# Windowed attention and two FFNs: float32 scores, and a new order of work around the transposes of P

## The chip, the cores and the metric

One core of one Trainium2 chip. The metric is the time of one execution on the device in microseconds. The engines are TensorE (PE in the profile, its weight loads PEld), VectorE (DVE), ScalarE (ACT), GpSimd (POOL) and SyncE (SP).

## What is computed

Sixteen heads (2 batches of 8) of 768 positions and 64 elements attend to the last 128 positions and to 4 sink positions at the start; the result, 1536 rows of 512, goes through two FFNs of width 2048. All inputs but the two sizes are float32 or float64, the output is float32.

```python
scores = scale * np.matmul(q, k.transpose(0, 1, 3, 2))
keep = (pos[None, :] < n_sink) | ((rel >= 0) & (rel < window))   # rel = query - key
scores = np.where(keep, scores, -1e9)
a = softmax(scores)
x = matmul(a, v)                       # to (B*S, H*D)
h = x @ w_in;  x = where(h >= 1, h, where(h <= -1, 0, (h + 1)**2 / 4)) @ w_out
h = x @ w2_in; out = (np.maximum(h, 0.0)**2) @ w2_out
```

## The kernel before

**Units.** Attention is cut into 24 units: a batch, a pair of heads `c` and a block `j` of 256 queries (`UNITS`). The two heads of a unit lie on partitions 0 to 63 and 64 to 127; a unit has two halves `u` of 128 queries. The steps of a unit are: loads of q and k (`q`) and of v (`v`); a key tile that takes over the last 128 keys and the sink columns of the block before (`k`, lines 366 to 375: one copy by SP's DMA queue, one POOL copy); the transposes of q and k on PE and their copies to SBUF (`t`, lines 377 to 398); the scores of each half with mask, maximum and exponential (`s0`, `s1`, lines 400 to 435); the norm (`n`, lines 437 to 453: an addition and a reciprocal on DVE, a product per half on POOL, and for j > 0 a small POOL copy per half of the probabilities of the sinks); the transposes of P for each head (`x0`, `x1`, lines 455 to 468) and of the sink columns (`xs`, lines 470 to 483, for j > 0 only), each copied out by ACT; and the product with V (`a`, lines 485 to 504), which for j > 0 begins with one matmul of the sink tile and then takes the two heads in turn, 64 columns of the array each.

**Number formats.** `turn` writes q and k transposed as two float32r parts: ACT casts the PSUM tile (line 394), DVE subtracts the cast from the tile (line 395). A head's scores are then three float32r matmuls (high x high, high x low, low x high: `SPLIT`), 64 rows of the array per head, heads taking turns (lines 410 to 419). A score block has 260 columns: 128 older keys, 4 sinks, 128 own keys; the first block of a sequence has 128. The product with V and all transposes are plain float32. The FFNs use float32r with the same split; their weights come as float64 and are split by ACT, DVE and POOL (`Weights.part`, lines 112 to 133).

**Order.** `fast_path` makes a list of events: step `nm` of unit `n` stands at `n + ORDER[nm]`; to it come the jobs that load or split FFN weights (`JOBS`: per key two loads, then two splits) and the first six FFN steps of 256 positions (`STEPS`). The list is sorted and issued; a planner then gives each engine its instructions by what is ready in its own reckoning, earlier events first. So FFN matmuls run between attention's from 34 us on. PSUM holds two score tiles (`SCB`), one of turned q and k, two of turned P, one for values and two for the FFN; SBUF holds four key tiles (`KB`), three units' P (`PB`) and two units' turned P (`PTB`). After attention the rest of the FFNs runs alone.

Of the kernel before, what the change touches and what calls it, by code (L numbers as in the profile page):

```python
# [8 lines left out]
F32 = mybir.dt.float32  # L9
F32R = mybir.dt.float32r  # L10
# [3 lines left out]
ALU = mybir.AluOpType  # L14
# [3 lines left out]
P = 128  # L18
# [7 lines left out]
NS = 4  # L26
WIN = 2 * P + NS
SLOT = P + NS
# [14 lines left out]
JOBS = [  # L43
    x + d
    for x in (
        3.64, 4.16, 4.68, 5.21, 5.73, 6.26,
        6.78, 7.30, 7.83, 7.83, 8.07, 8.31,
    )
    for d in (0, 0.01)
]  # L50
ORDER = dict(
    q=-1.74, k=-2.06, v=-1.14, s0=-0.59, s1=0.18, t=-0.86, n=1.23, x0=1.40, xs=1.69, x1=1.96, a=2.41,
)
STEPS = [
    (t, (n // 3, n % 3 * 256, 256)) for n, t in enumerate((13.7, 14.0, 17.6, 21.0, 21.2, 21.8))
]
CUTS = ((0, 2, 5, 8, 12, 16), (0, 4, 8, 12, 16))
PASSES = [
# [2 lines left out]
SPLIT = ((0, 0), (0, 1), (1, 0))  # L61


def f32(ap):
    return ap.bitcast(F32)
# [266 lines left out]
class Attention:  # L332
# [32 lines left out]

    def keys_before(self, b, j, c):
        nc = self.nc
        kt = self.po["k"].tile([P, 2, 5, SLOT], F32R, tag="k", name=f"k_{b}_{j}_{c}")
        if j > 0:
            old = f32(self.kt[b, j - 1, c])  # L370
            nc.sync.dma_start(f32(kt)[:, :, 0, :P], old[:, :, 2, :P])
            nc.gpsimd.tensor_copy(
                kt[:, :, 0:2, P:], old[:, :, 1, P:].unsqueeze(2).broadcast_to([P, 2, 2, NS])
            )
        self.kt[b, j, c] = kt

    def turn(self, b, j, c):
        nc, po, kt = self.nc, self.po, self.kt[b, j, c]
        banks = 2 if po["tag"] == "f" else 1
        ps = [  # L380
            po["tp"].tile([P, 4, P], F32, tag=po["tag"], name=f"tp_{b}_{j}_{c}_{i}")
            for i in range(banks)
        ]
        for a, src in enumerate("kq"):
            for u in range(2):
                nc.tensor.transpose(  # L386
                    ps[a % banks][:, 2 * a + u],
                    self.loads.raw[src, b, j, c][:, u].rearrange("p h d -> p (h d)"),
                    self.ident,
                )  # L390
        for i in range(banks):
            blocks = slice(4 * i // banks, 4 * (i + 1) // banks)
            src, dst = ps[i][:, blocks], kt[:, :, 1:, :P][:, :, blocks]
            nc.scalar.copy(dst[:, 0], src)
            nc.vector.tensor_tensor(dst[:, 1], src, f32(dst[:, 0]), ALU.subtract)
        if j == 0:
            nc.gpsimd.tensor_copy(kt[:, :, 1, P:], f32(kt[:, :, 1, :NS]))
        self.st[b, j, c] = dict(nm=f"{b}_{j}_{c}")

    def scores(self, b, j, c, u):  # L400
        nc, po, st = self.nc, self.po, self.st[b, j, c]
        kt = self.kt[b, j, c]
        keys = kt.rearrange("p s n w -> p s (n w)")
        k0 = SLOT if (j == 0 or u == 1) else 0
        wid = P if j + u == 0 else WIN
        ps = [
            po["sc"].tile([P, 512], F32, tag="s", name=f"s_{st['nm']}_{u}_{e}")[:, :wid]
            for e in range(2)
        ]
        for n, (a, bb) in enumerate(SPLIT):  # L410
            for e in range(2):
                pr = slice(64 * e, 64 * e + 64)
                nc.tensor.matmul(  # L413
                    ps[e],
                    kt[pr, a, 3 + u, :P],
                    keys[pr, bb, k0 : k0 + wid],
                    start=n == 0,
                    stop=n == 2,
                )
        if u == 0:  # L420
            st["p"] = [
                po["p"].tile([P, 2, WIN], F32, tag="p", name=f"p_{st['nm']}_{i}") for i in range(2)
            ]
            st["sm"] = po["sm"].tile([P, 3, 2, 2], F32, tag="sm", name=f"sm_{st['nm']}")
        s, sm = st["p"][u][:, :, :wid], st["sm"]
        mask = self.masks[min(2 * j + u, 2)][:, :wid]
        for e in range(2):
            nc.vector.tensor_tensor_reduce(  # L428
                s[:, e], ps[e], mask, -SCALE, 3.0e38, ALU.add, ALU.min, sm[:, 0, u, e : e + 1]
            )  # L430
        for e in range(2):
            nc.scalar.activation(  # L432
                s[:, e], s[:, e], AF.Exp, bias=sm[:, 0, u, e : e + 1], scale=-1.0,
                accum_out=sm[:, 1, u, e : e + 1],
            )
# [360 lines left out]
```

## Time and profile before

| | us |
|---|---|
| median of 3 runs | 685.02 (684.73 to 685.83) |
| profiled execution | 684.93 |
| its span | 682.8 |
| PE busy in the span | 666.5 |
| DVE, ACT, POOL busy | 426.0, 337.9, 295.7 |
| attention's last score matmul starts | 170.6 |
| the last matmul of a product with V starts | 182.1 |

Times in the rows count from the span's start. PE's printed durations reach from a matmul's start to its modelled end and overlap; what a group of matmuls takes from the engine is read from its start to the start of the next row. A plain float32 matmul stands in the trace as two records, a float32r one as one.

### The profile page before, as it was taken

How to read it: one execution, taken by the hardware profiler on the slowest of the kernel's cores; microseconds unless marked ns; L12 is line 12 of the kernel's file. 1: busy time of each engine (PE TensorE's matmuls, PEld its weight loads, DVE VectorE, ACT ScalarE, POOL GpSimd, SP SyncE). 2: the span in 40 equal slices, each digit the busy share in tenths (PEclk: the TensorE clock that was granted, in tenths of full speed). 3: DMA queues.
4: the chain of work that ended last, by engine and by line, in shares of the span. 5: the costliest groups of instructions: out<-in, count | busy, mean ns of one | idle time of the engine just before them, and what ended most of it. 6: DMA issues, size and time to landing. Idle time of an engine off the chain costs nothing.

```text
span 682.8 us, 9689 instructions
## 1 busy us (share of the span) xinstructions
PE 666.5 (98%) x3438; PEld 540.5 (79%) x3438; DVE 426.0 (62%) x885; ACT 337.9 (49%) x727; POOL 295.7 (43%) x302
## 2 busy tenths in 40 slices
PE   7989999999999999999999999999999999999996
PEld 5667777878888888888888878888888888888885
DVE  4788799675479777777677866663566356222221
ACT  4879787765455545445444555453444354122210
POOL 2365655444245444444436577353344344233111
PEclk7999999999999999999999999999999999999999
DMA  4857353210222222222211221221123010000111
GB/s 111 215 140 163 102 124 102 70 32 1 83 76 86 67 84 72 86 69 68 87 61 62 92 63 32 93 85 39 52 74 92 32 61 1 0 1 11 51 62 67
DMA packets 66393, 49.00 MB, mean 72 GB/s; under 512 B 40096, under 2 KB 60832, under 8 KB 66336
## 3 DMA queue, kind: packets, MB, share of 16 engines
q1 hardware_dynamic: 65792, 48.17, 24.5%
q8 instruction: 29, 0.48, 0.3%
q14 instruction: 28, 0.23, 0.1%
q10 hardware_dynamic: 544, 0.13, 0.1%
HBM read 43.04 MB, written 3.15 MB: 68 GB/s over the span
## 4 chain that ended last, share of the span: by engine, by line
PE 84%; DVE 6%; DMA 2%; POOL 2%; ACT 2%; issue 2%; SPq 1%; POOLq 0%; ACTq 0%; DVEq 0%
PE o L212 36%; PE h L178 34%; PE s L413 5%; PE av L501 4%; PE tx L463 3%; PE tp L386 1%; DVE t L187 1%; POOL x L223 1%; DVE wx L128 1%; SPq L322 1%; PE ts L476 1%; DVE u L188 1%; DMA wraw<-in_moe_w_in_dram 1%; POOL w L133 1%; DVE wx L126 1%
## 5 line engine op out<-in xcount | busy, mean ns | idle before, releaser
L178 PE MATMUL h<-x,w 128*128 128x512 f32 (+1 forms) x1272 | 277.7, 373 | 0.0
L178 PEld LDWEIGHTS h<-x,w 128*128 128x128 f32 x1272 | 224.5, 188 | 45.5 <-DVE sm L440 0.4
L212 PE MATMUL o<-g,w 128*128 128x512 f32 (+1 forms) x696 | 144.0, 359 | 1.9 <-POOL g L190 1.1
L133 POOL TENSOR_TENSOR w<-wx,w 128x512 fp32r<-128x512 f32 x64 | 83.3, 1302 | 134.2 <-ACT w L132 132.1
L212 PEld LDWEIGHTS o<-g,w 128*128 128x128 f32 x696 | 116.1, 188 | 25.4 <-POOL g L190 1.5
L212 PE MATMUL o<-w,g 128*128 128x512 f32 (+1 forms) x588 | 135.2, 389 | 0.0
L212 PEld LDWEIGHTS o<-w,g 128*128 128x128 f32 x588 | 109.0, 188 | 24.4
L196 POOL TENSOR_TENSOR g<-t,g 128x512 fp32r<-128x512 f32 x48 | 64.2, 1337 | 103.4 <-ACT g L195 86.7
L190 POOL TENSOR_TENSOR g<-u,g 128x512 fp32r<-128x512 f32 (+1 forms) x58 | 71.0, 1226 | 63.6 <-issue 31.1
L235 DVE TENSOR_TENSOR acc<-o,acc 128x512 f32<-128x512 f32 (+1 forms) x105 | 58.5, 577 | 59.0 <-PE o L212 58.8
L132 ACT CAST w<-wx 128x512 fp32r<-128x512 f32 x64 | 39.7, 621 | 94.9 <-DVE wx L131 75.2
L126 DVE TENSOR_SCALAR wx<-wx 128x512 f32<-128x512 f32 x64 | 38.2, 598 | 55.4 <-ACT wx L124 55.4
L194 DVE SCALAR_TENSOR_TENSOR t<-h,u 128x512 f32<-128x512 f32 x48 | 33.1, 689 | 63.0 <-ACT u L193 36.3
L448 POOL TENSOR_TENSOR p<-p,sm 128x520 f32<-128x520 f32 (+1 forms) x48 | 48.1, 1022 | 46.6 <-DVE sm L441 29.0
L193 ACT ACTIVATE u<-h 128x512 f32<-128x512 f32 x48 | 28.6, 596 | 66.6 <-PE h L178 66.6
L124 ACT ACTIVATE wx<-wraw 128x512 f32<-128x512 f32 x64 | 42.8, 669 | 33.5 <-POOL w L133 29.6
L128 DVE SCALAR_TENSOR_TENSOR wx<-wraw,wx 128x512 int32<-128x512 int32 x64 | 58.4, 913 | 1.0
L432 ACT ACTIVATE p<-p,sm 128x260 f32<-128x260 f32 (+1 forms) x96 | 47.4, 495 | 17.3 <-DVE sm L428 16.3
L187 DVE SCALAR_TENSOR_TENSOR t<-u 128x512 f32<-128x512 f32 (+1 forms) x58 | 43.5, 751 | 18.9 <-ACT u L186 18.9
L413 PE MATMUL s<-k 64*128 64x260 f32 (+1 forms) x288 | 50.3, 324 | 4.8 <-DVE sm L428 3.2
L428 DVE CUSTOM_DVE_ANT_0 p<-s,mask 128x260 f32<-128x260 f32 (+1 forms) x96 | 37.6, 401 | 25.5 <-PE s L413 21.3
L131 DVE CUSTOM_DVE_ANT_0 wx<-wx,wy 128x1024 uint16<-128x1024 uint16 x64 | 50.8, 794 | 1.2
(69 smaller groups left out, 595.5 us busy)
## 6 DMA issues: line engine op xcount, KB each, us to landing
wraw<-in_moe_w_in_dram SPq DMA_DIRECT2D x32, 512.0 KB
wraw<-in_moe_w_out_dram SPq DMA_DIRECT2D x32, 512.0 KB
vr<-in_v_dram SPq DMA_DIRECT2D x24, 128.0 KB
qr<-in_q_dram SPq DMA_DIRECT2D x22, 128.0 KB
kr<-in_k_dram SPq DMA_DIRECT2D x22, 128.0 KB
out_dram<-acc SPq DMA_DIRECT2D x11, 256.0 KB
k<-k SPq DMA_DIRECT2D x16, 128.0 KB
qr<-in_q_dram SPq DMA_DIRECT2D x4, 64.0 KB
```

The lines of the kernel that those rows point to most:

```text
L128: nc.vector.scalar_tensor_tensor(xi, hi, -(1 << 31), xi, ALU.bitwise_and, ALU.bitwise_or)
L131: nc.vector.tensor_tensor(xi, xi, yi, ALU.add)
L133: nc.gpsimd.tensor_tensor(w[:, 1], x, f32(w[:, 0]), ALU.subtract)
L178: nc.tensor.matmul(h, w[:, a, c * P : (c + 1) * P], x[:, b, c, sl], start=n == 0, stop=n == 11)
L187: nc.vector.scalar_tensor_tensor(t, u, 1.0, u, ALU.min, ALU.mult)
L190: nc.gpsimd.tensor_tensor(g[:, 1], u, f32(g[:, 0]), ALU.subtract)
L196: nc.gpsimd.tensor_tensor(g[:, 1], t, f32(g[:, 0]), ALU.subtract)
L212: nc.tensor.matmul(o, lhs, rhs, start=n == 0, stop=n == m - 1)
L235: self.nc.vector.tensor_tensor(dst, o, dst, ALU.add)
L413: nc.tensor.matmul(ps[e], kt[pr, a, 3 + u, :P], keys[pr, bb, k0 : k0 + wid], start=n == 0, stop=n == 2,)
L432: nc.scalar.activation(s[:, e], s[:, e], AF.Exp, bias=sm[:, 0, u, e : e + 1], scale=-1.0, accum_out=sm[:, 1, u, e : e + 1],)
L448: nc.gpsimd.tensor_tensor(s, s, r, ALU.mult)
```

## The change

The keys and queries are kept as one float32 tile: `turn` has one DVE copy out of PSUM in place of the cast on ACT and the subtraction on DVE, the copies of `keys_before` move half the bytes, and a head's scores are one float32 matmul, head 0 first. In the order of work x1 (the second head's transposes of P) comes next to x0, ahead of xs; the norm, x0, the keys, v and s0 move a little; the weight jobs come later, and one of the FFN steps changes its place.

```diff
--- before.py
+++ after.py
@@ -43,16 +43,16 @@
 JOBS = [
     x + d
     for x in (
-        3.64, 4.16, 4.68, 5.21, 5.73, 6.26,
-        6.78, 7.30, 7.83, 7.83, 8.07, 8.31,
+        4.00, 4.50, 5.05, 5.58, 6.10, 6.63,
+        7.15, 7.67, 8.20, 8.44, 8.68, 9.47,
     )
     for d in (0, 0.01)
 ]
 ORDER = dict(
-    q=-1.74, k=-2.06, v=-1.14, s0=-0.59, s1=0.18, t=-0.86, n=1.23, x0=1.40, xs=1.69, x1=1.96, a=2.41,
+    q=-1.74, k=-2.19, v=-1.12, s0=-0.63, s1=0.18, t=-0.86, n=0.94, x0=1.30, xs=1.94, x1=1.37, a=2.41,
 )
 STEPS = [
-    (t, (n // 3, n % 3 * 256, 256)) for n, t in enumerate((13.7, 14.0, 17.6, 21.0, 21.2, 21.8))
+    (t, (n // 3, n % 3 * 256, 256)) for n, t in enumerate((13.7, 14.0, 17.6, 21.7, 21.2, 22.0))
 ]
 CUTS = ((0, 2, 5, 8, 12, 16), (0, 4, 8, 12, 16))
 PASSES = [
@@ -365,12 +365,12 @@
 
     def keys_before(self, b, j, c):
         nc = self.nc
-        kt = self.po["k"].tile([P, 2, 5, SLOT], F32R, tag="k", name=f"k_{b}_{j}_{c}")
+        kt = self.po["k"].tile([P, 5, SLOT], F32, tag="k", name=f"k_{b}_{j}_{c}")
         if j > 0:
-            old = f32(self.kt[b, j - 1, c])
-            nc.sync.dma_start(f32(kt)[:, :, 0, :P], old[:, :, 2, :P])
+            old = self.kt[b, j - 1, c]
+            nc.sync.dma_start(kt[:, 0, :P], old[:, 2, :P])
             nc.gpsimd.tensor_copy(
-                kt[:, :, 0:2, P:], old[:, :, 1, P:].unsqueeze(2).broadcast_to([P, 2, 2, NS])
+                kt[:, 0:2, P:], old[:, 1, P:].unsqueeze(1).broadcast_to([P, 2, NS])
             )
         self.kt[b, j, c] = kt
 
@@ -390,33 +390,26 @@
                 )
         for i in range(banks):
             blocks = slice(4 * i // banks, 4 * (i + 1) // banks)
-            src, dst = ps[i][:, blocks], kt[:, :, 1:, :P][:, :, blocks]
-            nc.scalar.copy(dst[:, 0], src)
-            nc.vector.tensor_tensor(dst[:, 1], src, f32(dst[:, 0]), ALU.subtract)
+            nc.vector.tensor_copy(kt[:, 1:, :P][:, blocks], ps[i][:, blocks])
         if j == 0:
-            nc.gpsimd.tensor_copy(kt[:, :, 1, P:], f32(kt[:, :, 1, :NS]))
+            nc.gpsimd.tensor_copy(kt[:, 1, P:], kt[:, 1, :NS])
         self.st[b, j, c] = dict(nm=f"{b}_{j}_{c}")
 
     def scores(self, b, j, c, u):
         nc, po, st = self.nc, self.po, self.st[b, j, c]
         kt = self.kt[b, j, c]
-        keys = kt.rearrange("p s n w -> p s (n w)")
+        keys = kt.rearrange("p n w -> p (n w)")
         k0 = SLOT if (j == 0 or u == 1) else 0
         wid = P if j + u == 0 else WIN
         ps = [
             po["sc"].tile([P, 512], F32, tag="s", name=f"s_{st['nm']}_{u}_{e}")[:, :wid]
             for e in range(2)
         ]
-        for n, (a, bb) in enumerate(SPLIT):
-            for e in range(2):
-                pr = slice(64 * e, 64 * e + 64)
-                nc.tensor.matmul(
-                    ps[e],
-                    kt[pr, a, 3 + u, :P],
-                    keys[pr, bb, k0 : k0 + wid],
-                    start=n == 0,
-                    stop=n == 2,
-                )
+        for e in range(2):
+            pr = slice(64 * e, 64 * e + 64)
+            nc.tensor.matmul(
+                ps[e], kt[pr, 3 + u, :P], keys[pr, k0 : k0 + wid], start=True, stop=True
+            )
         if u == 0:
             st["p"] = [
                 po["p"].tile([P, 2, WIN], F32, tag="p", name=f"p_{st['nm']}_{i}") for i in range(2)
```

## Rows read from the trace of the kernel before

**Rows 1.** The page, part 1: busy us, share of the span, instructions.

```profile
PE 666.5 (98%) x3438; PEld 540.5 (79%) x3438; DVE 426.0 (62%) x885; ACT 337.9 (49%) x727; POOL 295.7 (43%) x302
```

**Rows 2.** Busy time by stage; columns: stretch, us, engines (instructions), PEclk, DMA share, GB/s.

```profile
0.00:20.00 20.00, 15.62 (x79) 12.60 (x80) 9.66 (x48) 8.38 (x25) 6.26 (x21) 0.74 0.56 127
20.00:45.00 25.00, 21.62 (x147) 15.49 (x147) 20.96 (x67) 21.91 (x66) 12.93 (x24) 0.95 0.67 177
45.00:187.00 142.00, 140.84 (x1039) 111.83 (x1036) 102.42 (x316) 99.95 (x284) 69.37 (x99) 1.00 0.34 86
187.00:675.00 488.00, 486.84 (x2167) 399.18 (x2166) 291.69 (x453) 207.71 (x354) 207.18 (x159) 1.00 0.19 59
```

**Rows 3.** Timeline of PE: start us, duration us, line, operation, tiles, shape, count.

```profile
22.11 0.84 PE L413 MATMUL s<-k 64*128 64x260 f32 x3
...
61.52 0.62 PE L413 MATMUL s<-k 64*128 64x260 f32 x3
62.08 0.44 PE L463 MATMUL tx<-ident,p 128*128 128x128 f32 x2
62.44 0.87 PE L501 MATMUL av<-pt,vr 128*64 128x256 f32 x8
63.24 0.74 PE L178 MATMUL h<-x,w 128*128 128x256 f32 x4
...
170.24 0.62 PE L413 MATMUL s<-k 64*128 64x260 f32 x3
```

**Rows 4.** Timeline of PE, 137.0 to 139.3 us.

```profile
137.04 0.64 PE L413 MATMUL s<-k 64*128 64x260 f32 x6
137.61 0.55 PE L463 MATMUL tx<-ident,p 128*128 128x128 f32 x3
137.91 0.36 PE L501 MATMUL av<-sink_t,vs 96*128 96x256 f32 x1
138.20 1.09 PE L501 MATMUL av<-pt,vr 128*64 128x256 f32 x12
139.22 0.55 PE L463 MATMUL tx<-ident,p 128*128 128x128 f32 x3
```

**Rows 5.** Timeline of PE, 152.3 to 155.4 us.

```profile
152.38 3.14 PE L178 MATMUL h<-x,w 128*128 128x256 f32 x24
155.36 0.38 PE L463 MATMUL tx<-ident,p 128*128 128x128 f32 x2
```

**Rows 6.** Timeline of PE, 109.3 to 112.3 us.

```profile
109.39 0.38 PE L501 MATMUL av<-sink_t,vs 96*128 96x256 f32 x1
109.71 0.65 PE L501 MATMUL av<-pt,vr 128*64 128x256 f32 x2
110.29 0.97 PE L212 MATMUL o<-g,w 128*128 128x256 f32 x6
111.19 1.08 PE L501 MATMUL av<-pt,vr 128*64 128x256 f32 x10
112.20 0.62 PE L413 MATMUL s<-k 64*128 64x260 f32 x3
```

**Rows 7.** Timeline of PE, 120.3 to 120.9 us.

```profile
120.36 0.55 PE L413 MATMUL s<-k 64*128 64x128 f32 x3
120.83 0.66 PE L463 MATMUL tx<-ident,p 128*128 128x128 f32 x4
```

**Rows 8.** Groups by line and shape: count, busy us, mean ns, idle before and releaser.

```profile
L395 DVE TENSOR_TENSOR k<-tp,k 128x512 fp32r<-128x512 f32 x23 | 15.6, 679 | 0.9 <-ACT k L394 0.9
L394 ACT CAST k<-tp 128x512 fp32r<-128x512 f32 x23 | 13.3, 579 | 4.0 <-PE tp L386 3.7 <-PE s L413 0.2
...
L233 DVE COPY acc<-o 128x512 f32<-128x512 f32 x16 | 10.7, 682 | 7.5 <-PE o L212 7.5
```

**Rows 9.** Timeline of PE, first and last broken product with V that has sinks.

```profile
76.62 0.36 PE L501 MATMUL av<-sink_t,vs 96*128 96x256 f32 x1
...
176.05 0.36 PE L501 MATMUL av<-sink_t,vs 96*128 96x256 f32 x1
```

**Rows 10.** Line 371 on SP: operation, count, duration ns min/median/max, first and last us.

```profile
L371 SPq EVENT_SEMAPHORE  x24: 17/28/5364, 8.4 to 129.2; - x24
```

## Prediction

> **What bounds the kernel now.** I read the page first: TensorE is marked busy 98% of the span [rows 1]. That alone does not say where an edit pays, so I cut the span by stage [rows 2]; the granted clock is 0.74 up to 20 us, a mix of 1.2 and 2.4 GHz, and 2.4 GHz from 45 us on. From 187 us to 675 us only the two FFN products run, 2167 matmuls in 488 us; the diff touches nothing there. Attention lies in the first 187 us. Up to 45 us TensorE is idle for 7.8 us (4.4 before 20 us, 3.4 after); from 45 us to 187 us it is idle for 1.2 us of 142, because FFN matmuls of the first steps fill every hole. DVE (102 us) and ACT (100 us) have room in that stage. So from 45 us on the time is the sum of what each visit to TensorE costs, and an engine beside it matters only where it changes how the visits fall.
>
> The third view is the order of TensorE's own work, where I take a visit's price from its start to the start of the next row (the printed durations overlap). Scores of one head, three float32r matmuls of 260 columns, cost 0.55 us [rows 3]. The scores of both heads, side by side in rows 0-63 and 64-127 of the array, cost 0.57 us together [rows 4]. Twenty-four FFN matmuls in a row cost 2.98 us, 0.124 each [rows 5], but six of them between two visits to a part of the array cost 0.90 us [rows 6] instead of 0.74. So a visit that splits in two pays its own fill and drain again and about 0.16 us more around it. This kernel is bound, in the stage that the diff touches, by the number of such visits.
>
> The Trainium skill, TensorEngine Tiling, section Key Properties, says that a change of tiling mode drains TensorE. The 0.90 against 0.74 us fits that; it adds no term of its own.
>
> **The score matmuls.** Removed: three float32r matmuls per head; added: one float32 matmul, which the trace shows as two records. No float32 matmul of 64 rows is in this trace. The nearest row is the float32 visit of one head in the product with V: two records of 256 columns, 0.58 us up to the next row [rows 6]. Four more columns and a 128-column weight load make it about 0.59, against 0.55: +0.035 us a visit. The trace has 37 visits of one head with 260 columns, the first at 22.1 us and the last at 170.2 [rows 3], and 16 of both heads as in [rows 4]: 53 x 0.035 = +1.9 us. For 128 columns, three records cost 0.47 us [rows 7]; two float32 transposes of 128 columns ahead of another part-array visit cost 0.36 [rows 3]. That is -0.11 us for ten visits, -1.1 us. The remaining heads' scores lie in early or broken visits; I leave them alone. The sum is +0.8 us.
>
> What could move it is whether float32 heads still run side by side. 0.58 less 0.36 is 0.22 for two records of 128 columns more, so a float32 record takes 0.11 us for each 128 columns. Eight records of the product with V would take 4 x 0.22 + 4 x 0.11 = 1.32 us in a row, and took 0.80 [rows 3]: in columns, float32 heads do share. If in rows they don't, the 16 joint visits cost 0.59 + 0.44 = 1.03 us for 0.57, +7.4 us. Below nothing only the 128-column visits lead, by 1.1 us: no row shows one head's float32 visit of 256 columns under 0.58. I take +0.8, since float32r scores already share by rows.
>
> The Trainium skill, FP8 and Floating Point Precision, section TensorE Precision Notes, says that true float32 takes four passes through the array. The two records of 0.22 us, beside 0.12 us for a float32r pass of as many columns, agree. By the rule alone, four passes for three, each of the 53 visits pays 0.12 us more, an estimate, +6.4 us; the row has less because a float32 visit waits less for its weights.
>
> **The keys.** Removed: the ACT cast of each turned tile, 23 of them of 579 ns [rows 8], 13.3 us, and with it one hop in the chain transposes, cast, subtraction, scores. The DVE subtraction (679 ns) becomes a DVE copy out of PSUM; the nearest such copy takes 682 [rows 8], so DVE is unchanged. The POOL copies of the sink columns and the SP copies of the old keys have half the bytes. From 45 us on, ACT's 13.3 us are hidden: TensorE has other work. From 20 to 45 us ACT is busy 21.9 of 25 us and DVE 21.0 [rows 2], so for the five units that pass there 5 x 0.58 = 2.9 us come off the fullest engine. Against it, up to 20 us the lower clock [rows 2] doubles what float32 streams more (0.44 for 0.36): +0.16 us for some six visits, +1.0. Bounds: -2.9 and +1.0 us; I take -1.0, the middle, since DVE is next to late there and keeps its work.
>
> **The order of work.** The numbers in ORDER are places in units; the planner issues what is ready, in this order. x1 (the second head's transposes of P) goes from 1.96 to 1.37, beside x0; xs (the sink columns) goes behind both, from 1.69 to 1.94; values stay at 2.41. Today the product with V often starts when only the first head's P is turned: sink and two records, then FFN work, then the other ten, 0.90 + 1.01 = 1.91 us [rows 6], where an unbroken visit takes 1.31 [rows 4]. With 0.16 for the fragment between, a broken product costs 0.76 us more. There are ten: seven with sinks, the first at 76.6 us and the last at 176.0 [rows 9], and three without. The product's first matmul needs the sink tile, which is now turned last, so both heads should be ready by then. I count six of the ten as mended: 6 x 0.76 = -4.6 us; bounds 0 and -7.6.
>
> The moved steps' other instructions: the norm (1.23 to 0.94) puts two small DVE and two to four POOL instructions ahead of the next unit's turn and second scores; POOL is busy 69 of 142 us [rows 2], so it is hidden. The keys step (-2.06 to -2.19) puts its SP copy ahead of the loads of V and 0.13 units nearer to the tile that it reads; SP's waits at that line are 28 ns in the median and 5.4 us at most [rows 10], and V is wanted over three units later: nothing. The jobs that load and split weights come 0.34 to 0.6 units later, the last pair 1.16. That takes splits out of the full stretch before 45 us and puts them where they are covered; FFN work has its first weights a little later. I count both at nothing. The steps that change places (21.7 before: 21.0) are filler at the end of attention, nothing.
>
> **Sum.** The profiled execution took 684.9 us with a span of 682.8, and the median of the runs is 685.0. 684.9 + 0.8 - 1.0 - 4.6 = 680.1. Own range 676 to 684.
>
> **The rivals.**
> *More joint visits.* Shorter keys and a freer order could let more scores find both PSUM banks free. Each pair of single visits that joins saves 0.55 + 0.55 + 0.16 - 0.59, about 0.7 us. Ten of 37 singles make five joint visits, all of them 18: -3.5 to -12.6 us, 667.5 to 676.6. For it: sixteen already find both banks free. Against it: the two banks still come free one DVE reduction after the other.
> *Broken visits (slower).* In the new cycle the next scores (0.37), x1 (0.37) and values (0.41) fall together behind x0 (0.30), all in different parts of the array, and a score bank is rarely free for two. If joint visits break, each costs 0.7 us; all 16 cost 11.2 us. From seven broken the gain is gone; with twelve it is 680.1 + 8.4 = 688.5. For it: singles already outnumber joint visits 37 to 16.
> *Float32 does not share the array by rows (slower).* +7.4 us on the sum, 687.5. A second road to the same place is that each visit pays its fourth pass in full, 53 x 0.12 + 10 x 0.06 = +7.0 in place of +0.8: 686.3. For both: no 64-row float32 matmul is in the trace. Against them: the 0.58 us row and the shared columns. (The second is what the Trainium skill's four passes would make of it: FP8 and Floating Point Precision, TensorE Precision Notes.)
> *The order does nothing.* The planner already starts what is ready; if the product breaks as often as now, only +0.8 and -1.0 remain: 684.7, or 685.7 with the early gain gone.
>
> **How the numbers follow.** The forecast has 0.44, more joint visits 0.14, broken visits 0.17, no sharing 0.10, nothing from the order 0.15. The likeliest is 680.1. Leaving out a tenth at each end, the range runs from 671 to 689. A measurement of this kernel tells about 0.2%, 1.4 us, from no change. Faster by more: 0.44 + 0.14, and 0.01 of broken visits with few breaks, 0.59. Within it: 0.12 of the last case and 0.04 of the middle of the others, 0.16. Slower: the rest, 0.25.
>
> **What would show it.** Right: the score visits have two records a head, 0.59 us alone and about 0.60 for both; no cast of k on ACT; fewer than five products with V in two pieces; the FFN-only stage begins about five microseconds earlier and is as long as now. Wrong: both heads' scores taking over 0.9 us, more score visits than now, idle TensorE beyond 45 us, or an end of attention at 187 us as today. The forecast fails above all if the planner's order of the visits changes in a way that the offsets do not tell.

## The result, and the profile after

The changed kernel takes 674.13 us (median of four, 673.47 to 674.81) against 685.42 for the kernel before beside it: a ratio of 0.983 (0.9815 to 0.9851), 11.3 us faster. The forecast was 680.1, so the sign and the range (671 to 689) held, and the gain was more than twice the 4.9 us that I had worked out. The profiled execution has a span of 671.7 us, against 682.8. Medians here and below are over all executions; ratios and their intervals leave out executions in a slower state (three of ten in e1, one of ten in e4, one of four in e10), and the traces of e1 and e10 are of such executions.

Page of the changed kernel, part 1, beside [rows 1]: the share of TensorE tells nothing again, 98% in both.

```profile
PE 658.9 (98%) x3342; PEld 525.4 (78%) x3342; DVE 426.2 (63%) x885; ACT 325.3 (48%) x702; POOL 296.9 (44%) x302
```

Busy time by stage, in the columns of [rows 2], cut just behind attention's end (176 us here, 187 there):

```profile
0.00:20.00 20.00, 16.10 (x70) 11.40 (x70) 11.04 (x50) 7.62 (x24) 6.92 (x21) 0.83 0.54 122
20.00:45.00 25.00, 24.80 (x157) 15.66 (x155) 20.28 (x72) 20.35 (x62) 12.94 (x23) 1.00 0.78 196
45.00:176.00 131.00, 129.24 (x926) 96.29 (x923) 101.70 (x308) 89.42 (x263) 69.35 (x101) 1.00 0.31 75
176.00:664.00 488.00, 486.79 (x2182) 400.27 (x2181) 291.47 (x453) 207.92 (x354) 207.71 (x159) 1.00 0.19 61
```

Three things differ. From 20 to 45 us TensorE was idle for 3.4 us and is for 0.2, at a granted clock of 1.00 in place of 0.95. From 45 us to the start of the last matmul of a product with V it took 137.1 us (to 182.1 us) and takes 128.6 (to 173.6). And in 488 us of the FFN-only stage, which I had left out of the sum, 2182 matmuls fit where 2167 did. The products with V in the changed kernel (count, duration in ns min/median/max, first and last start in us):

```profile
L494 PE MATMUL av<-pt,vr x256: 272/273/431, 18.5 to 173.6; 128*64 128x128 f32 x80, 128*64 128x256 f32 x48
```

Timeline of TensorE of the changed kernel: scores of both heads, then of one head; a whole product with V; one of 128 columns. Columns as in [rows 3].

```profile
61.77 0.71 PE L410 MATMUL s<-k 64*128 64x260 f32 x4
62.41 0.42 PE L469 MATMUL ts<-ident,sink_p 128*96 128x128 f32 x2
62.67 0.38 PE L456 MATMUL tx<-ident,p 128*128 128x128 f32 x2
63.00 0.70 PE L410 MATMUL s<-k 64*128 64x260 f32 x2
63.64 0.50 PE L178 MATMUL h<-x,w 128*128 128x256 f32 x2
...
86.37 0.55 PE L456 MATMUL tx<-ident,p 128*128 128x128 f32 x3
87.27 0.38 PE L494 MATMUL av<-sink_t,vs 96*128 96x256 f32 x1 [0.35 <-DVE sink_t L476]
87.58 1.09 PE L494 MATMUL av<-pt,vr 128*64 128x256 f32 x12
88.60 1.69 PE L212 MATMUL o<-g,w 128*128 128x256 f32 x12
...
117.93 0.48 PE L410 MATMUL s<-k 64*128 64x128 f32 x2
118.34 0.33 PE L456 MATMUL tx<-ident,p 128*128 128x128 f32 x1
```

From start to next start, one head takes 0.64 us (0.55 before, [rows 3]) and both heads also 0.64 (0.57, [rows 4]): float32 heads do share the array by rows. A head of 128 columns takes 0.41 (0.47, [rows 7]). The product with V from 87.27 us is whole and takes 1.33; its first row shows what it now waits for, the sink tile, which is turned last.

**Where the 11.2 us of the span went.** I gave each matmul of attention the time from its start to the next start, took recorded idle time out, and compared an FFN matmul inside attention with its 0.124 us [rows 5] for 256 columns (sums over all rows of both traces, us):

| | before | after | difference |
|---|---|---|---|
| scores | 45.3 | 46.9 | +1.6 |
| products with V, with sinks | 34.8 | 29.4 | -5.4 |
| FFN matmuls inside attention, above 0.124 each | 6.3 | 5.0 | -1.3 |
| transposes of the sink columns | 4.6 | 4.1 | -0.6 |
| other transposes, start | 39.8 | 40.1 | +0.3 |
| idle up to 20 us / 20 to 45 us / later | 2.7 / 3.4 / 1.2 | 2.2 / 0.2 / 1.8 | -0.5 / -3.2 / +0.6 |
| FFN-only stage, as much work | 500.6 | 497.9 | -2.7 |

Not all of the -5.4 for the products comes from their order. Two products in the kernel before were whole and dear: the one from 17.51 us took 1.51 us, where one of this kind (without sinks) takes 0.80 elsewhere, and the one from 44.03 us took 2.24, where 1.31 is usual. Both ran while the granted clock was 0.50, that is 1.2 GHz (first the timeline of TensorE, then busy time by stretch):

```profile
17.51 1.57 PE L501 MATMUL av<-pt,vr 128*64 128x256 f32 x8
19.02 0.50 PE L413 MATMUL s<-k 64*128 64x260 f32 x4
...
44.03 0.56 PE L501 MATMUL av<-sink_t,vs 96*128 96x256 f32 x1
44.52 1.81 PE L501 MATMUL av<-pt,vr 128*64 128x256 f32 x12
46.27 0.44 PE L463 MATMUL tx<-ident,p 128*128 128x128 f32 x2
```

```profile
14.00:18.00 4.00, 4.00 (x20) 3.14 (x22) 2.64 (x9) 2.33 (x7) 1.26 (x3) 0.50 0.42 100
43.00:46.00 3.00, 3.00 (x17) 2.37 (x19) 2.02 (x6) 1.92 (x4) 1.68 (x2) 0.50 0.86 256
```

That is 1.6 us of the 5.4. In the kernel after every product ran at 2.4 GHz. The rest, 3.7 us, is broken products: each of the ten before cost 0.57 us more than a whole one, 5.7 us in all, and the four after cost 2.0.

### The profile page after: what moved, and what is told of

Read it like the earlier page. It is cut to its first block, busy times and chain, and to the rows that moved or that the text cites. A ratio compares the mean times of both kernels' runs of the same rounds, so it can differ in the third digit from the quotient of the medians.

```text
span 671.7 us, 9449 instructions
## 1 busy us (share of the span) xinstructions
PE 658.9 (98%) x3342; PEld 525.4 (78%) x3342; DVE 426.2 (63%) x885; ACT 325.3 (48%) x702; POOL 296.9 (44%) x302
## 4 chain that ended last, share of the span: by engine, by line
PE 83%; DVE 7%; POOL 3%; ACT 2%; issue 2%; DMA 1%; SPq 0%; POOLq 0%; DVEq 0%; ACTq 0%
PE o L212 36%; PE h L178 34%; PE s L410 5%; PE av L494 3%; PE tx L456 3%; DVE wx L128 1%; PE tp L386 1%; POOL x L223 1%; DVE t L187 1%; DVE p L421 1%; POOL g L190 1%; DVE wx L127 1%; DVE wx L126 1%; DVE wx L131 1%; POOL w L133 1%
## 5 line engine op out<-in xcount | busy, mean ns | idle before, releaser
L441 POOL TENSOR_TENSOR p<-p,sm 128x520 f32<-128x520 f32 (+1 forms) x48 | 49.1, 1043 | 40.4 <-DVE sm L434 32.6
L131 DVE CUSTOM_DVE_ANT_0 wx<-wx,wy 128x1024 uint16<-128x1024 uint16 x64 | 48.8, 763 | 1.1
L189 ACT CAST g<-u 128x512 fp32r<-128x512 f32 (+1 forms) x58 | 31.4, 546 | 32.2 <-DVE u L188 31.2
```

Of the source, the lines that this page charges most:

```text
L131: nc.vector.tensor_tensor(xi, xi, yi, ALU.add)
L441: nc.gpsimd.tensor_tensor(s, s, r, ALU.mult)
```

## The experiments

Three numbers of each kernel come from the order of its matmuls: visits of the scores, how many of these hold one head alone or a part of one, and pieces in which the 24 products with V are done. Before: 77, 54, 34. After: 70, 47, 29. Times are medians, ratios go against the kernel before measured beside it. Two theories stood at the start: V, the forecast's (x1's place makes products with V whole, and the keys matter little), and K, that what decides is the keys' shorter chain.

**Halves of the change.** First the keys and scores alone (e1): the changed kernel with JOBS, ORDER and STEPS of before, of which ORDER stands here:

```diff
-    q=-1.74, k=-2.19, v=-1.12, s0=-0.63, s1=0.18, t=-0.86, n=0.94, x0=1.30, xs=1.94, x1=1.37, a=2.41,
+    q=-1.74, k=-2.06, v=-1.14, s0=-0.59, s1=0.18, t=-0.86, n=1.23, x0=1.40, xs=1.69, x1=1.96, a=2.41,
```

> The float32 keys and scores of the changed kernel with the tables ORDER, JOBS and STEPS of the kernel before: one part of the change alone. Theory V (the gain is fewer and whole visits to TensorE): in the order issued to TensorE this kernel has 75 score visits, 57 of them of one head, and 38 visits of the product with V (before: 77, 54 and 34; after: 70, 47 and 29), so no visit is saved, and each score visit is dearer by about 0.08 us (0.633 us after against 0.553 before): 75 x 0.08 = +6 less some 2 us of the early stretch, 686 to 690 us. Theory K (the shorter chain to the scores and the free ScalarE carry the gain): most of it is here already, 675 to 680 us.

Measured: 682.47 us, ratio 0.998 (0.995 to 1.001); 75, 57, 38. That lies between the ranges of the two theories. What the dearer visits cost is read from e4's trace below.

Then the tables alone (e2): the changed kernel with the keys and scores of before:

```diff
-        kt = self.po["k"].tile([P, 5, SLOT], F32, tag="k", name=f"k_{b}_{j}_{c}")
+        kt = self.po["k"].tile([P, 2, 5, SLOT], F32R, tag="k", name=f"k_{b}_{j}_{c}")
...
```

> The tables ORDER, JOBS and STEPS of the changed kernel with the float32r keys and scores of the kernel before: the other part alone. Theory V: 26 visits of the product with V (before 34) and 77 score visits as before: the product gains its 5.3 us and some for FFN pieces, 677 to 680 us. Theory K: the order alone gives little, 683 to 686 us.

Measured: 680.93 us, 0.994 (0.991 to 0.997); 77, 55, 26, a microsecond above theory V's range. Its ten executions spread from 676.2 us, at a mean granted clock of 0.994, to 683.7, at 0.978. The traced one took 681.25, at 0.988; busy time by stage, columns as in [rows 2]:

```profile
25.00:30.00 5.00, 4.65 (x23) 3.30 (x25) 4.12 (x16) 4.50 (x15) 1.94 (x4) 0.80 0.81 179
30.00:35.00 5.00, 4.33 (x21) 2.91 (x21) 2.51 (x9) 3.13 (x11) 1.84 (x2) 0.50 0.66 163
35.00:40.00 5.00, 4.48 (x24) 2.94 (x22) 2.49 (x10) 3.41 (x11) 3.20 (x5) 0.50 0.09 26
40.00:45.00 5.00, 4.99 (x37) 3.99 (x36) 1.94 (x9) 3.12 (x9) 2.51 (x7) 0.83 0.20 45
```

For some 13 us TensorE runs at 1.2 GHz, where the kernel after has 2.4 from 20 us on. So the halves, 2.2 and 3.7 us, don't add up to 11.3.

**x1 and xs alone**, in the kernel before (e3):

```diff
-    q=-1.74, k=-2.06, v=-1.14, s0=-0.59, s1=0.18, t=-0.86, n=1.23, x0=1.40, xs=1.69, x1=1.96, a=2.41,
+    q=-1.74, k=-2.06, v=-1.14, s0=-0.59, s1=0.18, t=-0.86, n=1.23, x0=1.40, xs=1.94, x1=1.37, a=2.41,
```

> The kernel before with two numbers changed: x1 1.96 to 1.37 and xs 1.69 to 1.94. It has 25 visits of the product with V, none in pieces, and 62 score visits, 29 of one head. Theory V: 9 visits of the product at 0.76 and 15 score visits at 0.7 us less, 685.4 - 6.8 - 10.5, 668 to 673 us, faster than the changed kernel without its keys. Theory K: no more than the product's pieces, 678 to 683 us.

Measured: 674.37 us, 0.987 (0.983 to 0.991); 62, 29, 25 (one product is still in two pieces). Two numbers of a table carry about as much as the whole change. Not only the products got whole (34 pieces to 25): the scores lost 15 visits. By the sums of the table above, scores fell by 5.4 us and products with V by 6.5.

The other side, all of the change but with the old ORDER (e4):

```diff
-    q=-1.74, k=-2.19, v=-1.12, s0=-0.63, s1=0.18, t=-0.86, n=0.94, x0=1.30, xs=1.94, x1=1.37, a=2.41,
+    q=-1.74, k=-2.06, v=-1.14, s0=-0.59, s1=0.18, t=-0.86, n=1.23, x0=1.40, xs=1.69, x1=1.96, a=2.41,
```

> The changed kernel with ORDER of the kernel before; JOBS and STEPS stay new. 77 score visits, 61 of one head, 39 of the product with V. Theory V: the gain is gone, 685 to 690 us. Theory K: most of it stays, 675 to 680 us. If JOBS and STEPS carried a part of it, this kernel is under the one with all three old tables by that part.

Measured: 683.62 us, 1.0005 (0.997 to 1.004); 77, 61, 39. That too lies between the two ranges. Idle from 20 to 45 us is 0.8 us here, so the early gain is there with the new keys and the old order too, and scores at 51.3 us (45.3 before) pay it back.

**Why do scores join?** A score bank is emptied by the DVE reduction that writes into P (line 428), and there are six P tiles, three units' worth. x1 holds them: until the second head is turned, its unit's two tiles are taken. Theory P: with x1 at 1.96 the next unit's scores found no P tile in the planner's reckoning, so that their banks came free one at a time and the heads went out singly. One tile more, and nothing else (e5):

```diff
-PB, PTB = 6, 4
+PB, PTB = 7, 4
```

> The kernel before with seven tiles for P in place of six; no order is touched. Theory P (a P tile is held until x1 has read it, so with x1 late the scores run out of P tiles, their score banks come free one at a time and the heads go singly): the issued order has 63 score visits, 31 of one head (before 77 and 54), and 32 visits of the product with V (before 34), still in pieces. 14 x 0.7 = -9.8 and -1 to -2 for the product: 673 to 677 us. Theory O (it is the place of x1 in the order that counts, through the product with V alone): 682 to 686 us.

Measured: 676.95 us, 0.988 (0.985 to 0.991); 63, 31, 32. Scores join as in e3 (40.4 us for 45.3) while products stay in pieces. Attention ends nine microseconds earlier than before (the last product's matmul started at 182.1 us), two of them because 18 fewer FFN matmuls lie inside it; that line in the groups of e5, with count, duration in ns min/median/max, first and last start:

```profile
L501 PE MATMUL av<-pt,vr x256: 272/273/690, 17.5 to 173.0; 128*64 128x128 f32 x79, 128*64 128x256 f32 x49
```

What is shown is that a seventh tile lets the planner join the scores. The step between, a reduction that waits for a tile, is not shown by the chip's own waits. DVE's waits for transposes of P before the reduction, from 45 to 187 us, of the kernel before and then of e5 (us, times, longest):

```profile
DVE p L428 <- PE tx L463: 2.3, 3, 1.2
```

```profile
DVE p L428 <- PE tx L463: 2.1, 2, 1.7
```

They hardly fall with the seventh tile, and e4, with six tiles and 61 single visits, has none.

The changed kernel with x1 back (e6):

```diff
-    q=-1.74, k=-2.19, v=-1.12, s0=-0.63, s1=0.18, t=-0.86, n=0.94, x0=1.30, xs=1.94, x1=1.37, a=2.41,
+    q=-1.74, k=-2.19, v=-1.12, s0=-0.63, s1=0.18, t=-0.86, n=0.94, x0=1.30, xs=1.94, x1=1.96, a=2.41,
```

> The changed kernel with x1 alone put back from 1.37 to 1.96. 80 score visits, 67 of one head (after: 70 and 47), 33 visits of the product with V, seven or eight in pieces (after 29). Theory V and P: +10 x 0.7 and +4 x 0.76, 674 + 10, 682 to 687 us: the whole gain hangs on this one number. Theory K (keys and the other numbers carry it): 674 to 678 us.

Measured: 687.62 us, 1.0038 (1.003 to 1.005); 80, 67, 33. The line of the products in it:

```profile
L494 PE MATMUL av<-pt,vr x256: 272/273/686, 19.2 to 186.1; 128*64 128x128 f32 x80, 128*64 128x256 f32 x48
```

The change without x1's place is slower than before: 57 whole visits of one head with 260 columns at 0.63 us and ten of both, where the kernel after has 41 and 17. All of the gain hangs on this number. TensorE was idle for only 0.1 us from 20 to 45 us here, at 2.4 GHz, so most of what it lost it lost in visits: scores took 53.3 us for 46.9, products 31.7 for 29.4.

**Are the two roads one?** If the shortage of P tiles is what x1 lifts, a seventh tile on top brings nothing. The same edit, in e3's kernel (e17) and in the changed one (e18):

```diff
-PB, PTB = 6, 4
+PB, PTB = 7, 4
```

> The kernel before with x1 at 1.37 and xs at 1.94 (674.4 us by an earlier run) and seven P tiles in place of six. Theory P (x1's earlier place pays by giving P tiles back earlier, which is what the seventh tile did alone, 8 us): the two gains are one and do not add. Issued visits of the scores 64, against 62 with six tiles: 673 to 676 us. Rival (they are two gains): 666 to 668 us.

> The changed kernel with seven P tiles. The order issued to TensorE is the same, matmul for matmul, as with six. Theory P: no P tile is short any more, so the time stays at 674.1 us, 673 to 675.5. Rival (the chip still waits for P tiles at places that the planner does not see): 2 us or more below, under 672 us.

Measured: 675.49 us (0.986; 64, 33, 24) and 675.73 us (0.987; 70, 47, 29). Neither gains: e18, whose order of matmuls is that of the kernel after, lies 0.2 us above the range that was expected. The two gains of 8 and 10 us are not two.

**Do fewer visits always pay?** Three score banks in place of two, the bank taken from the turned P, in the changed kernel (e7) and in e3 (e8):

```diff
-PSF, SCB, TPB, TXB, AVB = 2, 2, 1, 2, 1
+PSF, SCB, TPB, TXB, AVB = 2, 3, 1, 1, 1
```

> The changed kernel with three PSUM banks for scores and one for turned P in place of two and two. 54 score visits, 25 of one head (after 70 and 47); visits of the product with V 29 as after. Theory V: 16 x 0.7 = -11 us, 662 to 667 us. Rival (the one bank of turned P makes the transposes of one head wait for the copy of the other, and the time goes there): 672 to 680 us.

> The kernel before with x1 at 1.37, xs at 1.94 (674.4 us so) and three PSUM banks for scores, one for turned P. 57 score visits, 27 of one head (62 and 29 with two banks), 24 visits of the product with V (25). Theory V: -5 x 0.7 - 0.8, 669 to 672 us. Rival as in the run before this one: 674 to 680 us.

Measured: 695.28 us (1.014; 54, 25, 29) and 707.75 us (1.034; 57, 27, 24). I had this wrong. The fewest visits of all, and the longest times. Busy time from 45 to 170 us, e7 and then e8:

```profile
45.00:170.00 125.00, 118.26 (x823) 87.71 (x822) 94.47 (x295) 84.45 (x252) 63.15 (x93) 0.99 0.31 80
```

```profile
45.00:170.00 125.00, 112.44 (x845) 91.98 (x845) 94.05 (x279) 84.93 (x244) 61.27 (x85) 0.93 0.35 90
```

TensorE is idle for 6.7 and 12.6 us there (at granted clocks of 0.99 and 0.93), in the changed kernel for 1.8; up to the end of attention, which comes at 205 and 210 us, it is 12.6 and 18.3. Nor did e7's visits get cheaper in sum: its 54 visits of the scores took 46.0 us, the 70 of the kernel after 46.9. In e7 the waits of TensorE from 20 to 187 us name the transposes of P that wait for their single bank behind DVE (engine, line, waited for: us, times, longest):

```profile
PE tx L456 <- DVE sink_t L476: 4.7, 6, 1.1
PE s L410 <- DVE sm L421: 2.4, 4, 1.3
```

**The keys' copy on ACT** in place of DVE, in the changed kernel (e9):

```diff
-            nc.vector.tensor_copy(kt[:, 1:, :P][:, blocks], ps[i][:, blocks])
+            nc.scalar.copy(kt[:, 1:, :P][:, blocks], ps[i][:, blocks])
```

> The changed kernel with the one copy of the turned keys and queries on ScalarE in place of VectorE. 59 score visits, 26 of one head (after 70 and 47); 30 visits of the product with V (after 29). Theory V: 11 visits of 0.633 + 0.16 us less, 674 - 9 = 663 to 668 us, faster than both kernels. Theory E (the early gain came from taking the cast off ScalarE, the fullest engine before 45 us): the early stretch loses some 3 us again, and visits don't pay in full, 670 to 676 us.

Measured: 679.21 us, 0.988 (0.984 to 0.993); 59, 26, 30. A miss as well: eleven visits fewer than the kernel after, and 5 us slower. In this trace a load of keys by SP waited 8.5 us for transposes on TensorE to let its tile go, TensorE was idle for 6.0 us after 45 us, against 1.8, and it ran at 1.2 GHz from 30 to 40 us, with 30 matmuls where the changed kernel had 69. Which of these came first was not tried. Busy time by stage:

```profile
30.00:35.00 5.00, 5.00 (x16) 2.66 (x15) 1.31 (x7) 5.00 (x16) 3.39 (x5) 0.50 0.32 100
35.00:40.00 5.00, 5.00 (x14) 2.60 (x13) 1.99 (x9) 2.34 (x8) 0.61 (x4) 0.50 0.05 13
```

**The other entries.** The kernel before with x1, xs and s0 of the change, and its JOBS and STEPS (not shown; e10):

```diff
-    q=-1.74, k=-2.06, v=-1.14, s0=-0.59, s1=0.18, t=-0.86, n=1.23, x0=1.40, xs=1.69, x1=1.96, a=2.41,
+    q=-1.74, k=-2.06, v=-1.14, s0=-0.63, s1=0.18, t=-0.86, n=1.23, x0=1.40, xs=1.94, x1=1.37, a=2.41,
```

> The kernel before (float32r keys) with x1 at 1.37, xs at 1.94, s0 at -0.63 and the new JOBS and STEPS; n, x0, k and v stay. 60 score visits, 26 of one head, 25 visits of the product with V (the run with x1 and xs alone: 62, 29 and 25, 674.4 us). Theory V: 674.4 - 2 x 0.7, 671 to 674 us. If the later JOBS help the early stretch: down to 669; if they are what cost the run with all tables its early 4 us: 676 to 679 us.

The changed kernel with the old JOBS (e11):

```diff
-        4.00, 4.50, 5.05, 5.58, 6.10, 6.63,
-        7.15, 7.67, 8.20, 8.44, 8.68, 9.47,
+        3.64, 4.16, 4.68, 5.21, 5.73, 6.26,
+        6.78, 7.30, 7.83, 7.83, 8.07, 8.31,
```

> The changed kernel with JOBS of the kernel before: weights are loaded and split 0.34 to 1.16 units earlier. Score visits and visits of the product with V are as after (70, 47, 29). The prediction counted JOBS at nothing: 673 to 675 us. Rival: earlier splits fill VectorE and ScalarE before 45 us and hold the scores, 676 to 680 us.

And x1 and xs alone on float32 keys, the changed kernel with the old JOBS and STEPS and e3's ORDER (e12):

```diff
-    q=-1.74, k=-2.19, v=-1.12, s0=-0.63, s1=0.18, t=-0.86, n=0.94, x0=1.30, xs=1.94, x1=1.37, a=2.41,
+    q=-1.74, k=-2.06, v=-1.14, s0=-0.59, s1=0.18, t=-0.86, n=1.23, x0=1.40, xs=1.94, x1=1.37, a=2.41,
```

> Float32 keys and scores with the tables of the kernel before, but x1 at 1.37 and xs at 1.94: 72 score visits, 51 of one head, 30 visits of the product with V, three or four in pieces. The same two numbers with float32r keys gave 62, 29 and 25 and 674.4 us. Theory V: the early stretch gains 4 us, ten more visits cost 7, each of 72 visits is dearer by 0.08, 6: 680 to 685 us. Theory K: 668 to 673 us, the two gains add up.

Measured: 672.72 us (0.978, 0.973 to 0.984; 60, 26, 25), 675.09 us (0.984; 70, 47, 29) and 677.81 us (0.988; 72, 51, 30). JOBS is worth about a microsecond, less than the intervals tell apart. On e3's order float32 keys make ten visits more (e12). The ratios, 0.988 and 0.987, don't tell the two apart; e14 below, which is e3 with the FFN's tiles moved so that their matmuls go at e12's pace, takes 671.9 us, 6 us less than e12, and their intervals only just part. With the rest of the tables that cost is gone: the kernel after takes 674.1. Why float32 keys split visits in the planner's order was not tried.

**The FFN-only stage.** The diff touches nothing there, yet it is 2.7 us shorter in the kernel after. The mean time from one 512-column matmul to the next, without the few steps of 300 ns and more (3 to 6 of 2047), is 229.41 to 229.43 ns in the traces of the kernel after, e4, e6, e11 and e12, and 230.52 to 230.55 in those of the kernel before, e2, e3, e5 and e17: 1.1 ns x 2047 = 2.3 us. (The texts written ahead of the runs give the mean of all steps, 230.4 and 231.3.) The first have float32 keys, the others float32r. The first unit's key tile lies ahead of the FFN's tiles in SBUF, and is 2640 bytes smaller. Theory L: their addresses. An unused tile puts them back in the changed kernel (656 floats), or shifts them in the kernel before and in e3 (368). The runs are e13, e15 and e14, in this order:

```diff
+    one.tile([P, 656], F32, name="pad")
```

> The changed kernel with an unused tile of 2624 bytes a partition in the pool that holds the first unit's keys, so that all tiles behind it in SBUF, those of the FFN among them, lie where they lay before the change. Nothing else differs. Theory L (the FFN-only stage is 2.7 us shorter because its tiles lie elsewhere in SBUF): the mean slot of a 512-wide FFN matmul goes back from 230.4 to 231.3 ns, the stage behind attention grows by 2 to 2.7 us, the time is 676 to 677 us. Rival (it is shorter for another reason, for instance what attention leaves queued when it ends): slot and stage stay as in the changed kernel, 674.1 us.

> The kernel before with an unused tile of 1472 bytes a partition in the same pool, so that the FFN's tiles lie, in steps of 4096 bytes, as in the changed kernel. Nothing else differs. Theory L: the mean slot of a 512-wide FFN matmul falls from 231.3 to 230.4 ns and the time to 682.5 to 683.5 us. Rival: no change, 685.0 us.

> The kernel before with x1 at 1.37 and xs at 1.94 (674.4 us by an earlier run) and the same unused tile of 1472 bytes. Theory L: 672 to 673 us, slot 230.4 ns. Rival: 674.4 us, slot 231.3 ns.

Measured: 676.56 us (0.989), 682.62 us (0.997, 0.995 to 0.999) and 671.86 us (0.981, 0.977 to 0.985). The mean slots are 230.54, 229.42 and 229.42 ns. The group of the first product's matmuls from 187 to 660 us (busy us, mean ns; the duration printed), of the kernel before, e15, the kernel after and e13:

```profile
L178 PE MATMUL h<-x,w 128*128 128x512 f32 x1007 | 235.5, 392 | 0.0
```

```profile
L178 PE MATMUL h<-x,w 128*128 128x512 f32 x1015 | 235.7, 390 | 0.1
```

```profile
L178 PE MATMUL h<-x,w 128*128 128x512 f32 x998 | 231.5, 390 | 0.0
```

```profile
L178 PE MATMUL h<-x,w 128*128 128x512 f32 x1003 | 234.3, 392 | 0.0
```

The same instructions, in the same order on TensorE, have 392 or 390 ns by where their tiles lie. That is shown both ways; which tile matters, and why, is not.

**A candidate**, e14 with s0 at -0.63 (e16):

> The kernel before, float32r keys kept, with x1 at 1.37, xs at 1.94, s0 at -0.63 and the same unused tile: a candidate to beat both kernels. By the earlier run with the new places of the weight jobs and these three numbers (672.7 us) and by the finding that those places are worth about a microsecond: 672 to 674 us without theory L, 670 to 672 us with it.

Measured: 675.89 us, 0.988 (0.984 to 0.992); 60 visits of the scores, 25 pieces. A miss. The clock may be a part of it, which was not tried by itself: its executions have mean granted clocks of 0.975 to 0.980, e14's 0.987 to 0.999. Busy time by stage:

```profile
25.00:30.00 5.00, 4.06 (x30) 2.85 (x30) 4.72 (x17) 5.00 (x16) 1.01 (x3) 1.00 1.25 231
30.00:35.00 5.00, 4.65 (x26) 3.03 (x24) 2.41 (x9) 4.24 (x14) 3.37 (x5) 0.62 0.40 126
35.00:40.00 5.00, 5.00 (x20) 4.11 (x20) 1.45 (x7) 2.22 (x5) 2.54 (x6) 0.50 0.46 105
40.00:45.00 5.00, 5.00 (x25) 3.86 (x26) 2.61 (x10) 3.30 (x12) 0.66 (x5) 0.50 0.10 30
45.00:50.00 5.00, 5.00 (x26) 3.62 (x25) 3.92 (x14) 3.52 (x11) 4.14 (x8) 0.50 0.34 118
50.00:60.00 10.00, 9.29 (x70) 6.90 (x70) 7.65 (x27) 8.16 (x26) 3.89 (x6) 0.91 0.53 129
```

TensorE is idle for 0.9 us between 25 and 30 us, and then runs at 1.2 GHz for some 20 us, from 31 to 52, at 20 to 26 matmuls in 5 us; in e14's trace that stretch has 7 us. The best of all medians is e14's 671.86 us; its interval overlaps that of the kernel after, so it is not shown to beat it.

## Why the prediction was right or wrong

**What bounds the kernel.** Right in attention: the number and the wholeness of visits (e3, e5, e6). Wrong in one respect: e7 and e8, with fewer visits and 11 to 17 us more idle time beyond 45 us, show that this holds only while other work fills the holes.

**Which steps failed.** The sum gave -4.8 us, the span fell by 11.2. Scores and the order of work came out near their terms. Three steps did not: the early gain, put at -1.0 by the length of the cast, was 3.7 us of idle time; the FFN-only stage, put at nothing, gave 2.7; and the clock, which had no term, gave 1.6 in the products alone. Behind the sum a mechanism was missing as well: what x1's place does to the P tiles.

**Scores, +0.8 forecast, +1.6 measured.** Sharing by rows was right, and with it the main bound of +7.4 falls. The price was under-sized: +0.08 us a visit for the +0.035 that I took from the float32 visit of the product with V [rows 6], and -0.06 for 128 columns in place of -0.11. A price from another shape of visit was good to a twentieth of a microsecond, but the term is 58 visits long: by the measured prices alone it would be 58 x 0.08 - 10 x 0.06 = +4.0. That the sum came out near the forecast is in part luck: the other 2.4 came back, with seven visits fewer and none left that holds a part of a head. (The four passes of the Trainium skill, FP8 and Floating Point Precision, TensorE Precision Notes, would give +0.12 a visit, an estimate; the measured +0.08 is less.)

**The keys, -1.0 forecast.** The place was right, 20 to 45 us, and the size was not: idle time fell by 3.2 us there and by 0.5 before, more than my bound of -2.9. The step that failed is the price: I had counted the cast's own length on ACT. What went is idle time of TensorE behind the chain through DVE and the score banks. In that stretch the kernel before has this wait, and the kernel after none:

```profile
PE s L413 <- DVE sm L428: 2.6, 3, 1.6
```

Nor is it the keys' alone. The wait is 0.2 us in e4, which has the new keys and the old order, and 0.9 in e2 and 0.3 in e3, which have the old keys and x1 at its new place: either part takes most of it away, so the two gains overlap here too. (Idle time as a whole, 20 to 45 us, is 0.8 us in e4, 2.0 in e2 and 2.2 in e3.) And e1 and e4 show that the keys give no gain by themselves. e1's 2.2 us are no more than the shifted FFN tiles (2.3); in attention, e4's trace shows, the early gain goes into more and dearer visits.

**The order, -4.6 forecast, -5.0 measured** (broken products -3.7, FFN matmuls around them -1.3; the sinks' transposes, which I had not counted, -0.6). Mechanism, count and price were right: of ten broken products four are left, six mended, as I had counted. The step that failed lies beside this term: I gave x1's place nothing but the wholeness of products with V. It also gives back the P tiles, and the joining of scores I left to a rival with a chance of 0.14, to be caused by shorter keys. e3 and e5 show the joint visits come from x1 and the P tiles, 5 us of scores. In the change itself this is hidden, since float32 keys split as many visits again: 16 joint visits before, 17 after, and 10 with the keys but without x1 (e6). So the result of 674.1 us lies inside that rival's range (667.5 to 676.6), but not for the rival's reason.

**Nothing for the FFN-only stage** was another failed step: "the diff touches nothing there" was true of the code and not of the addresses. -2.7 us, of which 2.3 are shown to be placement.

**The clock was no term.** The kernel before has a granted clock of 0.76 from 40 to 45 us; the kernel after 1.00 from 20 us on. In the products that is worth 1.6 us, as shown above. e2 is the order without the keys: executions at 0.992 to 0.994 took 676.2 to 677.4 us, those at 0.978 683.4 to 683.7. If the former are free of the second slow stretch, 2.3 us of placement brings them to 674, where the kernel after lies. That would account for halves that don't add up. It is argued, not shown: only an execution at 0.988, with the stretch in it, has a trace. And the mean clock of an execution is a weak witness: in the traces of e2, e9 and e10 it counts as 1.00 up to 17.8 us and more, though two transposes of k at 5.71 us are marked 0.64 us in e2, where the kernel before has 0.40 at 2.4 GHz (5.45 us) and 0.69 at 1.2 (8.62 us); and e1's executions at 0.998 to 1.000 took 681.6 to 682.7 us, no less than those at 0.988 to 0.990 (681.5 to 682.3).

**The rivals.** That float32 heads don't share the array by rows is out: both take 0.64 us, as one does. That each visit pays its fourth pass in full is out too, at +0.08. Broken visits and an order that does nothing: out with x1, and without it e6 and e4 come close to these two cases, at 687.6 and 683.6 us. JOBS, STEPS and the other moved steps at nothing: right for JOBS within the noise (e11); the rest is open, since k, v, n and x0 were not moved one by one.

## What to carry to other kernels

In a planned order, ask of each moved step which buffers it gives back and who waits for these, before you ask what it makes whole: a place in a table and one more buffer may be the same remedy. Before a difference of a few tenths in a matmul group is put down to the order, look at the granted clock of its stretch. Two parts of a change that meet in one planner don't add up, so a sum of terms needs a rival for their meeting. And a tile that changes its size moves all tiles behind it, in stages that the diff doesn't touch.

## What was not expected of the hardware

The same 512-column float32r matmuls took 229.42 or 230.54 ns each (steps of 300 ns and more left out), by nothing but the addresses of their tiles, to within 0.03 ns in nine traces at the one value and in six at the other. And a little idle time of TensorE before 45 us was followed by a second stretch at 1.2 GHz in several kernels: in e2 it was idle for 0.8 us between 20 and 30 us and then slow for some 13 us; in the kernel after it was idle for 0.2 us and stayed at 2.4 GHz. e4, e11, e13 and e18, with 0.2 to 0.8 us of idle time from 20 to 45 us, have no second stretch either; e12, e14 and e17, with 1.6 to 3.1 us, have one. Against it stand e9, idle for 0.8 us as e4 is, but slow from 28 to 42 us, and e3, idle for 2.2 us without a second stretch, though its first lasts longer (0.72 from 20 to 25 us). Whether idle time is the cause was not tried by itself.
